# Two mixture-of-experts layers behind a windowed attention: the first weight matrix, the second group's softmax and the residues of the last two weight jobs are put in another order at the end of the preparation

## The chip, the cores and the metric

The kernel runs on one core of one Trainium2 chip. The time is device microseconds (us) of one execution; "the time before" is the median of three runs. A profile of one execution gives the rows below.

## What is computed

`x` is [2, 3584, 192]. Each token first gets a softmax-weighted mean over a window of seven rows (8 heads, `weight_gen`). Then a mixture of 8 experts with the best two of eight by noisy logits, then a second one with the best one by cosine similarity:

```python
w = exp(weight_gen - max); w = w / (sum(w) + 1e-9)
x = einsum('bshk,bskhg->bshg', w, windows_of(x))        # 7 rows back
for e in range(8):                                      # layer one, top 2 of 8
    h = maximum(x[mask] @ w1[e], 0); out[mask] += gate * (h @ w2[e])
# layer two: top 1 of 8, out[mask] = gate_w * (relu(x @ w1[e]) @ w2[e])
```

There are 7168 tokens, 192 features, 1024 hidden features. All inputs are fp32; the kernel forms fp16 pairs (a high part and a residue) to keep the precision.

## The kernel before, in words

**Stages.** The kernel has a head, in which no expert product runs, and a body, in which tiles of 256 tokens of one expert go through TensorE one after the other. The 56 columns of 128 tokens are cut into three groups: columns 0 to 24, 24 to 40 and 40 to 56. The head does the attention, the gate and the list of rows of the first group, and the preparation of layer one's weights. The attention and the lists of the other groups run on VectorE and ScalarE beside the tiles of the body.

**Weight jobs.** `prep_gen` (L308) prepares the weights of a layer in eight jobs of two experts each: four for the first matrix `w1` (m == 0) and four for the second matrix `w2` (m == 1). A job loads fp32 weights into one of three staging places (the end of `xh`, and the two weight buffers `wb`, called wb_134 and wb_133 in the built program), sums squares on ScalarE (`junk`), gets a scale `wsc` by a small matmul and VectorE steps (`wss`, `q`, `wsc`, `wiv`, `cinv`), and then for each half forms the high part on ScalarE (L395, `wo`) and the residue on VectorE (L397, `wo`). Each job of `w2` has four such pairs of 768 columns and two writes of 768 KB to the DRAM table `ws` (L404). The jobs are counted 0 to 7 here; job 5 uses wb_133, job 6 the end of `xh`, job 7 wb_134.

**First list.** `ctl` for the first group ends in `list_gen` (L835) and `decode` (L903): VectorE forms one-hot factors (`ol`, `ou`, `orr`), TensorE multiplies them (L875), VectorE reads the product (`dv`, L897) and goes by `va`, `dfv`, `sx`, `df` to the index table `gx` (L912). That last step is kept in `state["ctl"]`. GpSimd's indirect gathers of token rows (`xg`, L1123) wait for it.

**Second group's softmax.** `softmax_gen` (L433) does the largest of seven, subtraction, exponential on ScalarE (L442), sum, reciprocal and multiplication on `wt`. For the second group its first step is put behind `state["ctl"]`. Its input comes by `load_w(*G1[1])`, issued in the setup at priority `R_B`.

**First tile.** For each tile TensorE transposes the gathered rows (L1164, `pt`), ScalarE copies them (L1168, `xt`), and `first_product` (L1173) does four groups of ten matmuls into `ph`, a PSUM tile with three buffers. After each group ScalarE writes the high part `hh` (L1190) and VectorE the residue `hl` (L1191), which frees the `ph` buffer. Behind each half of the first tile's transposes, 18 small matmuls (`warm`, L1149) run. The second tile's transposes are issued behind the third group. `second_product` (L1198) then multiplies `hh` and `hl` by the second matrix into `py` (L1211).

**Weights of a tile.** `weights` (L1139) has SyncE read the expert number and a flag from tables in SBUF (`xi`, `fi`) and issue the load from `ws` into `wb` (L1147): part 0 is the first matrix (1024 KB), part 1 the second (768 KB). All loads and stores of SyncE stand in one queue, in the order in which it issues them; an issue that waits holds all issues behind it.

**What sets the order.** The kernel is written as generators that a queue steps; a scheduler orders the instructions of each engine by priorities (`p0 + R_CTL` is the most urgent; then `R_ATT`, `R_PREP`, `R_B`, `R_BODY`) and by `tc.issue_after`, which keeps an instruction behind a named one.

Of the kernel before, what the change touches and what calls it, by code (L numbers as in the profile page):

```python
# [12 lines left out]
ALU = mybir.AluOpType  # L13
AX = mybir.AxisListType

N, D, E, F, H, G, K = 7168, 192, 8, 1024, 8, 24, 7
# [3 lines left out]
G1 = ((0, 24), (24, 40), (40, 56))  # L20
# [7 lines left out]
CJ = 2  # L28
R_CTL, R_ATT, R_PREP, R_B, R_BODY = 0, 2000, 2000, 18000, 20000
C_AT = 5  # L30
R_LOW = 40000
P_STEPS = (0.5, 1.0)
SHARE = 0.845
ORDER = (0, 0, 1, 0, 1, 0, 1, 1)
# [51 lines left out]
def two_moe(ctx: ExitStack, tc: tile.TileContext, x, wgen, w_gate, w_noise, noise, w1a, w2a, emb, tau, w1b, w2b, out):  # L86
# [6 lines left out]
    WS = [[nc.dram_tensor(f"ws{i}{j}", (E * 128, n), F16, kind="Internal").ap() for j, n in enumerate((4096, WC - 4096))] for i in range(2)]  # L93
# [8 lines left out]
    V, A, PE, SP, PL = nc.vector, nc.scalar, nc.tensor, nc.sync, nc.gpsimd  # L102
# [28 lines left out]
    wr = wgen.rearrange("b s h k -> (b s) (h k)").rearrange("(p t) c -> p t c", t=NCOL)  # L131

    def load_w(a, b):
        SP.dma_start(wt[:, a:b].rearrange("p t h k -> p t (h k)"), wr[:, a:b])

    def load_x(a, b):
        SP.dma_start(xh[:, 6 + a:6 + b], xr[:, a:b])
# [140 lines left out]
    assert G1[0][1] * D >= 3072 and (G1[1][1] - G1[0][1]) * D >= 3072  # L278

    ready = set()  # L280

    @contextmanager
    def urgent(l):
# [9 lines left out]
    side, state = [], {"tile": 0}  # L293
# [14 lines left out]
    def prep_gen(l, w1, w2):  # L308
# [28 lines left out]
        for i, (e, m) in enumerate(jobs):  # L337
# [32 lines left out]
            n = 2  # L370
# [9 lines left out]
            for c in range(3 if m == 0 else 2):  # L380
                if len(wos) > 2 and any(f is wos[-3] for f, _ in side):
                    flush(True)
                wo = prep.tile([128, 3072], F16, name="wo", bufs=3)
                if m == 0:
                    n = 2048
                    w = 512 if l else 1024
                    pieces = [(wo[:, f:f + w], wo[:, 1024 + f:1024 + f + w], st[:, 1024 * c + f:1024 * c + f + w]) for f in range(0, 1024, w)]
                else:
                    n = 3072
                    wv = wo.rearrange("p (g a d) -> p g a d", a=2, d=D)  # L390
                    sv = st[:, 1536 * c:1536 * c + 1536].rearrange("p (g d) -> p g d", d=D)
                    w = 2 if l else 4
                    pieces = [(wv[:, g:g + w, 0], wv[:, g:g + w, 1], sv[:, g:g + w]) for g in range(0, 8, w)]
                for h, lo, v in pieces:
                    A.activation(h, v, AF.Copy, scale=sc[:, c:c + 1])  # L395
                    yield 0.1
                    V.scalar_tensor_tensor(lo, v, sc[:, c:c + 1], h, op0=ALU.mult, op1=ALU.subtract)  # L397
                    yield 0.6
                    if not l:
                        yield 0.1  # L400
                        yield 0.5
                def write(e=e, m=m, c=c, wo=wo, n=n):
                    if m == 1:
                        SP.dma_start(WS[l][1][(e + c) * 128:(e + c + 1) * 128], wo)  # L404
                    elif c < 2:
                        SP.dma_start(WS[l][0][(e + c) * 128:(e + c + 1) * 128, 0:2048], wo[:, 0:n])
                    else:
                        for q in range(4):
                            r = (e + q // 2) * 128 + 64 * (q % 2)
                            SP.dma_start(WS[l][0][r:r + 64, 2048:4096], wo[64 * (q // 2):64 * (q // 2) + 64, 0:n])  # L410

                wos.append(write)
                if l:
                    behind(write, 1)
                else:
                    write()
# [16 lines left out]
    def softmax_gen(a, b):  # L433
        n = (b - a) * H
        w = wt[:, a:b].rearrange("p t h k -> p (t h) k")
        m = ranks[1][0].rearrange("p e c -> p (e c)")
        with (tc.issue_after(state["ctl"].ins) if a == G1[1][0] else ExitStack()):
            V.tensor_reduce(m[:, :n], w, axis=AX.X, op=ALU.max)
        yield 6.0e-3 * n
        V.tensor_tensor(w, w, m[:, :n, None].to_broadcast([128, n, K]), op=ALU.subtract)  # L440
        yield 6.0e-3 * n
        A.activation(w, w, AF.Exp)  # L442
        yield 0.5
        V.tensor_reduce(m[:, :n], w, axis=AX.X, op=ALU.add)
        V.tensor_scalar(m[:, :n], m[:, :n], 1e-9, None, op0=ALU.add)
        V.reciprocal(m[:, :n], m[:, :n])
        yield 12.0e-3 * n
        V.tensor_mul(w, w, m[:, :n, None].to_broadcast([128, n, K]))
        yield 6.0e-3 * n

    state.update(accs=0, att=0)
# [671 lines left out]
            PL.indirect_dma_start(out=xg[:, h], out_offset=None, in_=T[l][0:rows_in],  # L1123
                                      in_offset=bass.IndirectOffsetOnAxis(ap=gidx[l][:, u + h:u + h + 1], axis=0))

    loads = []
    lone = [[i for i in seq if tiles[i][0] == l and tiles[i][4] == 1] for l in range(2)]

    def lone_weights(i):
# [43 lines left out]
    def first_product(i, bg):  # L1173

        l, L, pos, u, nh = tiles[i]
        c, w = slot(i)
        n = 128 * nh
        xm, xl, xr3 = live[i]["xt"]
        hh, hl = hidden[turn[i]]

        for g in range(4):
            ph = psum.tile([128, 2, 256], F32, name="ph", bufs=3)
            for q in range(2):
                f = 2 * g + q
                a, b, r, r2 = (w[:, o + 128 * f:o + 128 * f + 128] for o in (0, 1024, 2048, 3072))
                ops = ((a, xm), (a, xl), (b, xm), (r, xr3), (r2, xr3))
                for j, (s, m) in enumerate(ops):
                    state["pe"] = mark = PE.matmul(ph[:, q, :n], s, m, start=j == 0, stop=j == 4)  # L1188
            fs = slice(2 * g, 2 * g + 2)
            A.activation(hh[:, fs, :n], ph[:, :, :n], AF.Relu)  # L1190
            state["pin"] = V.scalar_tensor_tensor(hl[:, fs, :n], ph[:, :, :n], 0.0, hh[:, fs, :n], op0=ALU.max, op1=ALU.subtract)  # L1191
            bg(SHARE * nh / 2)
            if g == 2 and after.get(i) in live:
                with tc.issue_after(mark.ins):
                    transp(after[i])
            yield
        live[i]["h"] = (hh, hl)
# [88 lines left out]
    def att_gen(g):  # L1286
        a, b = L1.groups[g]
        while g and not ctl_done.get("h") or g == 2 and not state.get("last"):
            yield None
        cuts = [a, a + CH, b] if g == 0 else [a, b]  # L1290
        for u, v in zip(cuts, cuts[1:]):
            yield from softmax_gen(u, v)
        while g and head["on"]:
            yield None
        for c0 in range(a, b, CH):
            acc = yield from (att_chunk(c0) if g else att_chunk_pe(c0))
            bgq.chain(post_chunk(0, acc, c0, lgs[0][g], a, None, dones[0][g]))
        state["att"] += 1
# [127 lines left out]
    bgq.chain(prep_gen(0, w1a, w2a), "h", p0 + R_PREP)  # L1426
    load_x(2 * CH, GA)
    tc.cur_priority = p0 + R_B
    load_w(*G1[1])
    load_x(*G1[1])  # L1430
    tc.cur_priority = p0
    bgq.rank = p0 + R_CTL
# [4 lines left out]
        bgq.add(0, ctl(1, g, f"c{g}"), f"c{g}")  # L1437
    bgq.add(1, att_gen(0), "h", 0, p0 + R_ATT)
    for g in range(1, len(G1)):
        bgq.add(1, att_gen(g), f"s{g}")  # L1440
    bgq.add(1, emb_prep(), "c0")
    bgq.add(2, prep_rest(), "c0", 0, p0 + R_LOW)
    for g, (a, b) in enumerate(G2):
        bgq.add(1, combine_gen(g), f"c{g}", run_by(b))
    bgq.finish("h")
    head["on"] = False
    assert not locks["rows"]
    limit["rows"] = 1
# [33 lines left out]
        gather(i)  # L1482
    for part in range(2):
        for i in seq[:2]:
            weights(i, part)
    transp(0)
    for _ in first_product(0, bgq.point):
        pass
# [69 lines left out]
```

## Time and profile before

| | us |
|---|---|
| median of three runs | 1017.2 (1016.65 to 1022.86) |
| the profiled execution | 1016.67 |
| its span, first to last instruction | 1014.9 |
| TensorE busy in the span | 889.3 (88%) |
| VectorE busy | 682.5 (67%) |
| ScalarE busy | 572.3 (56%) |
| granted TensorE clock, mean | 0.963 of full |

The profiled execution took 1.77 us more than its span. In the rows, PE is TensorE's matmul, DVE is VectorE, ACT is ScalarE, POOL is GpSimd, SP is SyncE. A row of the timeline has the start from the beginning of the span, the duration, the engine and line, what is written and read, and in brackets the idle time before it and what ended that. Several instructions of one kind in succession are merged to one row (x4), with the time from the first's start to the last's end.

### The profile page before, as it was taken

How to read it: one execution, taken by the hardware profiler on the slowest of the kernel's cores; microseconds unless marked ns; L12 is line 12 of the kernel's file. 1: busy time of each engine (PE TensorE's matmuls, PEld its weight loads, DVE VectorE, ACT ScalarE, POOL GpSimd, SP SyncE). 2: the span in 40 equal slices, each digit the busy share in tenths (PEclk: the TensorE clock that was granted, in tenths of full speed). 3: DMA queues.
4: the chain of work that ended last, by engine and by line, in shares of the span. 5: the costliest groups of instructions: out<-in, count | busy, mean ns of one | idle time of the engine just before them, and what ended most of it. 6: DMA issues, size and time to landing. Idle time of an engine off the chain costs nothing. (4 is left out here: it accounts for less than half of the span.)

```text
span 1014.9 us, 26141 instructions
## 1 busy us (share of the span) xinstructions
PE 889.3 (88%) x9750; PEld 802.8 (79%) x9750; DVE 682.5 (67%) x1732; ACT 572.3 (56%) x1219; POOL 400.3 (39%) x379
## 2 busy tenths in 40 slices
PE   4993149999899999999899789899999989999995
PEld 2552139998889988889888688898898889999995
DVE  8996959998998958973457668275866663323331
ACT  2978526677557668356756774366357434434442
POOL 1000043454354544553544434354455334443532
PEclk9997559999999999999999999999999999999998
DMA  8789792856288584759999976782886657387650
GB/s 258 200 250 284 253 347 90 255 174 198 81 271 282 173 288 150 234 197 298 322 365 359 325 248 219 266 307 78 267 279 243 208 170 246 122 333 257 211 184 23
DMA packets 96393, 236.32 MB, mean 233 GB/s; under 512 B 13439, under 2 KB 64223, under 8 KB 87808
## 3 DMA queue, kind: packets, MB, share of 16 engines
q1 hardware_dynamic: 79360, 200.35, 58.0%
q0 software_dynamic: 16896, 34.20, 10.9%
q8 instruction: 79, 1.29, 0.5%
q14 instruction: 58, 0.48, 0.1%
HBM read 230.60 MB, written 57.90 MB: 284 GB/s over the span
## 5 line engine op out<-in xcount | busy, mean ns | idle before, releaser
L1188 PE MATMUL ph<-xt,wb 128*128 128x256 f16 x3360 | 413.6, 274 | 17.7 <-DMA wb<-ws 7.3
L1188 PEld LDWEIGHTS <-wb 128*128 128x128 f16 x3360 | 324.0, 98 | 57.1 <-issue 13.2
L1211 PE MATMUL py<-wb,hh 128*128 128x192 f16 x2688 | 357.5, 247 | 10.1 <-issue 5.4
L1190 ACT ACTIVATE hh<-ph 128x512 f16<-128x512 f32 (+1 forms) x368 | 209.3, 577 | 243.5 <-PE ph L1188 125.8
L1211 PEld LDWEIGHTS <-hh 128*128 128x128 f16 x2816 | 252.4, 98 | 20.5 <-issue 16.6
L1123 POOL DMA_INDIRECT xg<-t,gx x176 | 186.5, 1060 | 191.1 <-DVE gx L912 124.6
L1219 POOL DMA_INDIRECT yb<-ys,sx x116 | 130.8, 1128 | 250.9 <-ACT ys L1216 231.2
L1191 DVE SCALAR_TENSOR_TENSOR wt<-ph,hh 128x512 f16<-128x512 f32 x184 | 126.3, 688 | 144.5 <-ACT hh L1190 108.2
L1191 DVE SCALAR_TENSOR_TENSOR hl<-ph,hh 128x512 f16<-128x512 f32 (+1 forms) x184 | 117.6, 641 | 141.4 <-ACT hh L1190 113.3
L1211 PE MATMUL py<-wb,wt 128*128 128x192 f16 x736 | 181.9, 247 | 2.9 <-issue 2.9
L1211 PE MATMUL py<-wb,hl 128*128 128x192 f16 x608 | 149.5, 246 | 2.1 <-issue 2.0
L1219 POOL DMA_INDIRECT out_dram<-ys,sx x60 | 61.5, 1025 | 134.4 <-ACT ys L1216 120.5
L1216 ACT ACTIVATE ys<-py,xg 128x192 f32<-128x192 f32 x176 | 64.6, 415 | 64.3 <-PE py L1211 50.5
L465 DVE TENSOR_TENSOR tmp<-xh,wt 128x768 f32<-128x768 f32 x90 | 84.7, 951 | 1.4 <-PE ph L492 1.0
L1168 ACT ACTIVATE xt<-pt 128x768 f16<-128x768 f16 x84 | 67.9, 808 | 29.5 <-remote 12.3
L1211 PEld LDWEIGHTS <-wt 128*128 128x128 f16 x736 | 72.3, 98 | 3.8 <-issue 3.6
L1211 PEld LDWEIGHTS <-hl 128*128 128x128 f16 x672 | 65.7, 98 | 1.0 <-issue 0.9
L1164 PE MATMUL pt<-identh,xg 128*128 128x128 f16 x528 | 45.2, 220 | 11.1 <-DMA xg<-t,gx 9.7
L395 ACT ACTIVATE wo<-xh,wsc 128x384 f16<-128x384 f32 (+3 forms) x66 | 44.2, 716 | 12.5 <-DVE wsc L264 12.1
L397 DVE SCALAR_TENSOR_TENSOR wo<-xh,wsc,wo 128x384 f16<-128x384 f32 (+3 forms) x66 | 48.6, 744 | 2.9 <-ACT wo L395 2.8
L559 ACT ACTIVATE xt<-rb 128x768 f16<-128x768 f16 x56 | 43.4, 812 | 10.7 <-PE rb L553 4.9
L1164 PEld LDWEIGHTS <-xg 128*128 128x128 f16 x528 | 36.4, 98 | 13.6 <-DMA xg<-t,gx 10.3
(330 smaller groups left out, 918.3 us busy)
## 6 DMA issues: line engine op xcount, KB each, us to landing
wb<-ws SPq DMA_DIRECT2D x84, 1024.0 KB
wb<-ws SPq DMA_DIRECT2D x84, 768.0 KB
ws<-wo SPq DMA_DIRECT2D x16, 768.0 KB
tmp<-yb SPq DMA_DIRECT2D x28, 384.0 KB
ws<-wo SPq DMA_DIRECT2D x16, 512.0 KB
ws<-wo SPq DMA_DIRECT2D x32, 256.0 KB
xh<-ws SPq DMA_DIRECT2D x8, 1024.0 KB
xh<-in_moe_w_dram SPq DMA_DIRECT2D x10, 768.0 KB
```

The source lines that it names most:

```text
L395: A.activation(h, v, AF.Copy, scale=sc[:, c:c + 1])
L397: V.scalar_tensor_tensor(lo, v, sc[:, c:c + 1], h, op0=ALU.mult, op1=ALU.subtract)
L465: V.tensor_mul(dst.rearrange("p t (h g) -> p (t h) g", g=G), xv, w)
L1123: PL.indirect_dma_start(out=xg[:, h], out_offset=None, in_=T[l][0:rows_in], in_offset=bass.IndirectOffsetOnAxis(ap=gidx[l][:, u + h:u + h ...
L1164: mark = PE.transpose(pt[:, j, h], xg[:, h, 128 * b:128 * b + 128], identh)
L1168: A.activation(xt.rearrange("p j h n -> p (j h n)"), pt.rearrange("p j h n -> p (j h n)"), AF.Copy)
L1188: state["pe"] = mark = PE.matmul(ph[:, q, :n], s, m, start=j == 0, stop=j == 4)
L1190: A.activation(hh[:, fs, :n], ph[:, :, :n], AF.Relu)
L1191: state["pin"] = V.scalar_tensor_tensor(hl[:, fs, :n], ph[:, :, :n], 0.0, hh[:, fs, :n], op0=ALU.max, op1=ALU.subtract)
L1211: state["pe"] = PE.matmul(py[:, h], t[:, f, hs], w2[:, f, c], start=f == 0 and j == 0, stop=f == 7 and j == 2)
L1216: A.activation(ys[:, h], py[:, h], AF.Copy, scale=xg[:, h, 192:193].bitcast(F32))
L1219: d = PL.indirect_dma_start(out=dst, out_offset=bass.IndirectOffsetOnAxis(ap=sidx[l][:, u + h:u + h + 1], axis=0), in_=ys[:, h], in_offset ...
```

## The change

Six edits stand in the diff.
1. The residues of layer one's last two weight jobs (6 and 7) are held until the first list is there and put behind `state["ctl"]`. The last residue is kept as `state["wlast"]`.
2. The second group's softmax is put behind `state["wlast"]`, and starts only when layer one's weights are all prepared; all of it is written in the head, at the rank `R_SOFT`.
3. Its last multiplication is kept as `state["smax"]`, and the first tile's residues `hl` are put behind that.
4. The load of the second group's `weight_gen` columns is issued behind the write of job 5's second half, and stands in `loads`, the list behind whose last member the next weight load is put.
5. The first tile's first matrix is loaded at rank `R_CTL`, the other three loads of the first two tiles at `R_BODY + 1000`.
6. `loads` is made earlier, and `load_w` returns the instruction.

```diff
-R_LOW = 40000
+R_LOW, R_SOFT = 40000, 8000
...
     def load_w(a, b):
-        SP.dma_start(wt[:, a:b]...
+        return SP.dma_start(wt[:, a:b]...
...
+                    last = not l and i >= len(jobs) - 2
+                    while last and "ctl" not in state:
+                        yield None
+                    with tc.issue_after(state["ctl"].ins) if last else ExitStack():
+                        mark = V.scalar_tensor_tensor(lo, v, sc[:, c:c + 1], h, op0=ALU.mult, op1=ALU.subtract)
+                    if not l:
+                        state["wlast"] = mark
...
                     if m == 1:
-                        SP.dma_start(WS[l][1][(e + c) * 128:(e + c + 1) * 128], wo)
+                        mark = SP.dma_start(WS[l][1][(e + c) * 128:(e + c + 1) * 128], wo)
+                        if (l, e, c) == (0, 2, 1):
+                            with tc.issue_after(mark.ins):
+                                loads.append(load_w(*G1[1]))
...
-        with (tc.issue_after(state["ctl"].ins) if a == G1[1][0] else ExitStack()):
+        with (tc.issue_after(state["wlast"].ins) if a == G1[1][0] else ExitStack()):
             V.tensor_reduce(m[:, :n], w, axis=AX.X, op=ALU.max)
...
-        V.tensor_mul(w, w, m[:, :n, None].to_broadcast([128, n, K]))
+        state["smax"] = V.tensor_mul(w, w, m[:, :n, None].to_broadcast([128, n, K]))
...
-            state["pin"] = V.scalar_tensor_tensor(hl[:, fs, :n], ph[:, :, :n], 0.0, hh[:, fs, :n], op0=ALU.max, op1=ALU.subtract)
+            with tc.issue_after(state["smax"].ins) if i == seq[0] else ExitStack():
+                state["pin"] = V.scalar_tensor_tensor(hl[:, fs, :n], ph[:, :, :n], 0.0, hh[:, fs, :n], op0=ALU.max, op1=ALU.subtract)
...
+        while g and 0 not in ready:
+            yield None
         for u, v in zip(cuts, cuts[1:]):
             yield from softmax_gen(u, v)
+        state["soft"] = g
...
-    load_w(*G1[1])
...
-        bgq.add(1, att_gen(g), f"s{g}")
+        bgq.add(1, att_gen(g), f"s{g}", 0, p0 + R_SOFT)
...
     bgq.finish("h")
+    while state["soft"] < 1:
+        bgq.threads[1][0].step()
...
         for i in seq[:2]:
+            tc.cur_priority = p0 + (R_CTL if (i, part) == (seq[0], 0) else R_BODY + 1000)
             weights(i, part)
+    tc.cur_priority = p0 + R_BODY
```

**VectorE, end of the first list.** `wo<-xh` are residues of job 6, `dv` to `gx` the last steps of the list, `wss` the first scale step of job 7. Before:

```order
L885 TENSOR_TENSOR ou<-jtab,rhf 128x4x128
L397 SCALAR_TENSOR_TENSOR wo<-xh,wsc,wo 128x4x192
L886 TENSOR_TENSOR orr<-ou,vtab 128x4x128
L397 SCALAR_TENSOR_TENSOR wo<-xh,wsc,wo 128x4x192
L897 TENSOR_SCALAR dv<-ph 128x64
L397 SCALAR_TENSOR_TENSOR wo<-xh,wsc,wo 128x4x192
L1007 CAST va_186<-dv 128x64
L368 TENSOR_REDUCE wss<-pt 128x2
```

With the change (the lines are those of the changed file, ten or so further down):

```order
L895 TENSOR_TENSOR ou<-jtab,rhf 128x4x128
L896 TENSOR_TENSOR orr<-ou,vtab 128x4x128
L907 TENSOR_SCALAR dv<-ph 128x64
L1017 CAST va_186<-dv 128x64
L916 TENSOR_SCALAR dfv<-va_186 128x34
L919 CAST sx_172<-dfv 128x34
L920 TENSOR_SCALAR dfv<-dfv 128x34
L921 TENSOR_SCALAR df_1217<-dfv 128x34
L922 TENSOR_TENSOR gx_170<-dfv,df_1217 128x34
L402 SCALAR_TENSOR_TENSOR wo<-xh,wsc,wo 128x4x192 x4
L369 TENSOR_REDUCE wss<-pt 128x2
```

The four residues of job 6 moved from between the list's last steps to behind `gx`; job 7's four then follow, and the softmax (L448 to L458) follows those, ahead of the first `hl`.

**ScalarE, first tile.** `wo<-wb_134` are the high parts of job 7, `wt<-wt` is the softmax's exponential, `xt<-pt` the copies of the first and the second tile's transposes, `hh_190<-ph` the first tile's high parts. Before:

```order
L347 ACTIVATE junk,wnr<-wb_134 128x768
L395 ACTIVATE wo<-wb_134,wsc 128x4x192 x4
L442 ACTIVATE wt<-wt 128x896
L1168 ACTIVATE xt<-pt 128x768
L1190 ACTIVATE hh_190<-ph 128x512 x3
```

With the change:

```order
L396 ACTIVATE wo<-wb_134,wsc 128x4x192
L1177 ACTIVATE xt<-pt 128x768
L1199 ACTIVATE hh_190<-ph 128x512
L396 ACTIVATE wo<-wb_134,wsc 128x4x192
L1199 ACTIVATE hh_190<-ph 128x512 x2
L1177 ACTIVATE xt<-pt 128x768
L452 ACTIVATE wt<-wt 128x896
L1199 ACTIVATE hh_190<-ph 128x512
```

Two high parts of job 7 stand at each of the two L396 rows' places. Job 7's second half moved behind the first tile's first `hh`, and the exponential behind three `hh` and the second tile's `xt`.

**SyncE, first weight loads.** `ws<-wo` are the weight jobs' writes, `wb_133` takes the first tile's matrices, `wb_134` the second's. Before:

```order
L134 DMA wt<-in_weight_gen_dram 128x896
L404 DMA ws<-wo 128x3072 x2
L137 DMA xh<-in_x_dram 128x3072
L404 DMA ws<-wo 128x3072 x2
L1145 TENSOR_LOAD xi_166
L1147 DMA wb_133<-ws 128x4096
L1147 DMA wb_134<-ws 128x4096
L1147 DMA wb_133<-ws 128x3072
```

With the change (in both, the small register rows between the loads are left out):

```order
L134 DMA wt<-in_weight_gen_dram 128x896
L1154 TENSOR_LOAD xi_166
L1156 DMA wb_133<-ws 128x4096
L411 DMA ws<-wo 128x3072 x4
L137 DMA xh<-in_x_dram 128x3072
L1156 DMA wb_134<-ws 128x4096
L1156 DMA wb_133<-ws 128x3072
```

The first tile's first matrix moved ahead of four `ws` writes and the load of `x`; the load of `x` moved behind the last `ws` write, just ahead of the second tile's first matrix.

## Rows read from the trace of the kernel before

**Rows 1.** Waits of TensorE over the span (total us, times, longest).
```profile
PE pt L1164 <- DMA xg<-t,gx: 9.7, 1, 9.7
PE ph L1188 <- DMA wb<-ws: 7.3, 2, 6.1
```

**Rows 2.** Timeline of PE, 120 to 157 us.
```profile
125.04 0.59 PE L875 MATMUL ph<-orr,ol 128*128 128x64 bf16 x8 [1.95 <-DVE orr L886]
...
135.82 0.50 PE L1164 MATMUL pt<-identh,xg 128*128 128x128 f16 x3 [9.67 <-DMA xg<-t,gx]
...
137.87 1.65 PE L1154 MATMUL ph<-identh 128*128 128x96 f16 x18
145.64 6.23 PE L1188 MATMUL ph<-xt,wb 128*128 128x256 f16 x30 [6.12 <-DMA wb<-ws]
...
152.04 2.47 PE L1188 MATMUL ph<-xt,wb 128*128 128x256 f16 x20
...
156.43 0.82 PE L1188 MATMUL ph<-xt,wb 128*128 128x256 f16 x6
```

**Rows 3.** Timeline of DVE, 90 to 175 us.
```profile
122.38 1.01 DVE L397 SCALAR_TENSOR_TENSOR wo<-xh,wsc,wo 128x768 f16<-128x768 f32 x1
123.30 0.42 DVE L885 TENSOR_TENSOR ou<-jtab,rhf 128x512 bf16<-128x512 bf16 x1
...
125.83 0.22 DVE L897 TENSOR_SCALAR dv<-ph 128x64 int32<-128x64 int32 x1
...
128.00 0.20 DVE L912 TENSOR_TENSOR gx<-dfv,df 128x34 int32<-128x34 f32 x1
...
132.89 1.08 DVE L444 TENSOR_REDUCE rk<-wt 128x128 f32<-128x896 f32 x1
...
136.05 1.09 DVE L448 TENSOR_TENSOR wt<-wt,rk 128x896 f32<-128x896 f32 x1
148.62 0.69 DVE L1191 SCALAR_TENSOR_TENSOR hl<-ph,hh 128x512 f16<-128x512 f32 x1 [11.47 <-ACT hh L1190]
```

**Rows 4.** Timeline of ACT, 126 to 149 us.
```profile
127.62 3.42 ACT L395 ACTIVATE wo<-wb,wsc 128x768 f16<-128x768 f32 x4 [1.69 <-DVE wsc L264]
131.15 0.95 ACT L442 ACTIVATE wt<-wt 128x896 f32<-128x896 f32 x1
138.12 0.81 ACT L1168 ACTIVATE xt<-pt 128x768 f16<-128x768 f16 x1 [6.02 <-PE pt L1164]
147.99 0.60 ACT L1190 ACTIVATE hh<-ph 128x512 f16<-128x512 f32 x1 [9.06 <-PE ph L1188]
```

**Rows 5.** Timeline of SP's issues, 110 to 142 us (x2: first start to last end).
```profile
118.22 0.42 SPq L134 DMA_DIRECT2D wt<-in_weight_gen_dram  x1
124.68 2.66 SPq L404 DMA_DIRECT2D ws<-wo  x2
127.39 0.42 SPq L137 DMA_DIRECT2D xh<-in_x_dram  x1
...
132.07 3.22 SPq L404 DMA_DIRECT2D ws<-wo  x2
137.97 0.37 SPq L1147 DMA_DIRECT2D wb<-ws  x1
139.85 2.33 SPq L1147 DMA_DIRECT2D wb<-ws  x2
```

**Rows 6.** Timeline of POOL: the first gather.
```profile
128.49 1.14 POOL L1123 DMA_INDIRECT xg<-t,gx  x1 [124.56 <-DVE gx L912]
```

**Rows 7.** Windows: stretch, length, busy of PE, PEld, DVE, ACT, POOL, granted clock, DMA share, GB/s.
```profile
122.00:124.00 2.00, 0.58 (x8) 0.47 (x8) 2.00 (x5) 2.00 (x4) 0.00 (x0) 0.50 0.21 82
...
140.00:142.00 2.00, 0.00 (x0) 0.00 (x0) 0.00 (x0) 0.00 (x0) 1.41 (x2) 0.50 1.06 283
...
145.60:151.30 5.70, 5.66 (x27) 4.04 (x28) 2.68 (x4) 1.19 (x2) 0.00 (x0) 0.50 0.89 357
151.40:245.00 93.60, 93.60 (x1089) 88.49 (x1088) 89.40 (x150) 62.38 (x140) 44.08 (x36) 1.00 0.58 183
```

More of the change, by code (lines that the diff above doesn't have):

```diff
@@ L133, in load_w @@
     def load_w(a, b):
-        SP.dma_start(wt[:, a:b].rearrange("p t h k -> p t (h k)"), wr[:, a:b])
+        return SP.dma_start(wt[:, a:b].rearrange("p t h k -> p t (h k)"), wr[:, a:b])
     def load_x(a, b):
@@ L280, in two_moe @@
     ready = set()
+    loads = []
     @contextmanager
@@ L396, in prep_gen @@
                     yield 0.1
-                    V.scalar_tensor_tensor(lo, v, sc[:, c:c + 1], h, op0=ALU.mult, op1=ALU.subtract)
+                    last = not l and i >= len(jobs) - 2
[5 more added lines that the diff above has]
+                        state["wlast"] = mark
                     yield 0.6
@@ L1124, in gather @@
                                       in_offset=bass.IndirectOffsetOnAxis(ap=gidx[l][:, u + h:u + h + 1], axis=0))
-    loads = []
     lone = [[i for i in seq if tiles[i][0] == l and tiles[i][4] == 1] for l in range(2)]
```

## The prediction, made before the changed kernel ran

> **What bounds the kernel now.** The view of the waits comes first, since TensorE is busy for 88% of the span and its idle time is what can be won. Its two long waits on data are both at the hand-over from head to body: 9.7 us for the first gathered rows (`pt <- xg`) and 6.1 us for the first weights (`ph <- wb`) [rows 1]. The timeline of PE shows them one behind the other: the last product of the first list runs at 125.04, the transposes at 135.82, the warm-up ends at 137.87 + 1.65 = 139.5, and the first tile's product starts at 145.64 [rows 2]. The stretch from 125.6 to 145.6 holds 4 us of PE work.
>
> The other timelines say why. On DVE the index table `gx` comes at 128.00, with residues of job 6 among the list's last steps [rows 3]; the gather starts 0.49 us later [rows 6]. On SP the first matrix of the first tile is issued at 137.97, since it stands behind the weight jobs' last write, the second of the two issues that start at 132.07 and end at 135.29 [rows 5]. The windows show half clock (0.50) from the hand-over to 151.3, then full clock [rows 7]. From 151.4 to 245 us PE is busy without a gap that counts [rows 7], so whatever lead the first two tiles have there is carried on.
>
> **The change part by part.**
>
> *The list (edit 1).* A residue takes 123.30 - 122.38 = 0.92 us of DVE's time [rows 3]. Three of job 6 stand ahead of `dv`, one behind it. Without them the last two one-hot steps would run from 122.38 to about 123.1, TensorE's last eight matmuls take 0.59 [rows 2], and `dv` starts near 123.9 instead of 125.83, now bound by that product. From `dv` to `gx` it was 128.00 - 125.83 = 2.17, of which one residue goes: 1.2. So `gx` starts at 125.1, 2.9 us earlier, and the first gather at 125.6.
>
> *The gather.* Before, the transposes came 135.82 - 128.49 = 7.3 us after its start [rows 2, 6]. This trace has no row for that gather on a free queue. Two `ws` writes of 768 KB and the 1536 KB load of `x` were issued from 124.68 to 127.81 [rows 5], 3.1 MB, some 9 us of DMA at the 357 GB/s of a full stretch [rows 7], so the gather ran into them. Now one write of 768 KB goes out beside it, at about 127.2. The bounds are 1.1 (the gather's own time) and 7.3; I take 3.5, since the bytes ahead shrink by three quarters. Transposes then start at 129.1, and the warm-up ends 3.7 later, at 132.8.
>
> *The first matrix (edits 4 and 5).* Its issue follows the `wt` load, 118.22 + 0.42, and the register reads, which took 137.97 - 135.29 = 2.7 [rows 5]: 121.3. DMA is nearly empty there, 82 GB/s between 122 and 124 [rows 7]. The 448 KB of `wt` and 1024 KB at 357 GB/s take 4.2, so it lands by 126, and the 6.1 us wait for weights is gone. What is late next is the gather and ScalarE's copy `xt`. The copy now stands behind job 7's first two high parts. Those need `wsc`, behind job 6's four residues: 125.3 + 3.7 + 0.6 (three dependent steps of 0.2, as `gx`) = 129.6, and 2 x 0.86 (a quarter of 3.42, [rows 4]) end at 131.3. The copy waits for both, about equally long, and the product starts at 133.0, 12.6 us earlier than at 145.64.
>
> *What gives most of it back (edits 1 to 3).* The first `hl` is now behind the softmax, and on ScalarE the exponential stands behind `hh` one to three and the second tile's `xt`, with job 7's second half behind the first `hh`. TensorE's fourth group needs the buffer that the first `hl` frees. Step by step: a group takes 6.23 / 3 = 2.1 at half clock, so `hh` one runs at 135.2 to 135.8; job 7's two high parts to 137.5; DVE forms their residues to 138.6, then two softmax steps of 1.0 each to 140.6. ScalarE meanwhile does `hh` two and three (the third group ends at 139.3), then the second `xt` at 140.0 to 140.8. The exponential follows (0.95), to 141.8. The four steps behind it took 136.05 + 1.09 - 132.89 = 4.25 with one residue between them, 3.3 without [rows 3]: 145.1. With 0.7 for the first `hl`, the fourth group starts at 145.9, against 152.04 [rows 2]. Of 12.6 us, 6.1 are left, and TensorE is idle from 139.8 to 145.9.
>
> *The weights behind it.* Job 7's last write is issued when its last residue is done, 138.7; then comes the load of `x` (0.42), then the second tile's first matrix, 2.7 later, then the first tile's second matrix 1.9 later (139.85 - 137.97). The queue holds 0.79 + 1.57 + 1.05 = 3.4 MB up to the second tile's first matrix and 4.2 MB with the next. At 360 GB/s (the better of the two full windows, 283 and 357 [rows 7]) and with 1 us from issue to movement, they land at 149.2 and 151.4. Before, the load of `x` was out of the way by 135.
>
> *The clock.* Before, the product ran at half clock from 145.64 to 151.3, after 6.1 us of idle [rows 2, 7]. I take the same for the fourth group, since it too follows a gap of 6 us. Then: fourth group 145.9 to 148.0, wait for weights to 149.2, first group of the second tile to 151.3, full clock from about 152, second group to 152.8, twelve `py` matmuls to 153.8. The third group of the second tile starts at 153.8 instead of 156.43 [rows 2]: 2.6 us earlier. The Trainium skill says, in "TensorE: Matmul & The Clock Gate", section "Why this matters for your kernels", that an idle gap between bursts of matmuls sends the array back to half clock; it speaks against this change, which cuts the first product in two. The trace agrees, with 0.50 after the idle 139.5 to 145.6. Were the clock full throughout, the second matrix at 151.4 would bind and the lead be 4.0; were it half to 155, the lead would be 1.
>
> *The rest.* VectorE's lead at the first `hl` is 148.62 - 145.1 = 3.5, more than 2.6, so it does not become the bound. The order of later work stays: the second list's `gx` stands behind 63 residues `hl` instead of 62, the third's behind 123 in both. I cost that at nothing; TensorE's products hide it, and it is worth 2 us either way if they don't. Edit 6 costs nothing.
>
> The sum is 1016.67 (the profiled execution, 0.5 under the median of 1017.2) - 2.6 = 1014.1 us.
>
> **The rivals.**
> 1. *The whole head start stays.* If something lets the exponential run early, all 12.6 us are won: 1004.1. The early product and the free queue at 122 speak for it; the order on ScalarE, where the exponential stands behind the third `hh`, speaks against it, and no engine reorders its own list.
> 2. *Slower, by the late gather.* If the gather takes its old 7.3 us, the transposes start at 132.9 and the product at 136.8. Job 7's second half hangs on the first `hh`, so its last write moves to 142.5, and the load of `x` and both weight loads behind it: the second matrix lands at 155.2. At half clock twelve `py` end at 157.2 to 158.6, 0.8 to 2.2 later than 156.43, so 1017.5 to 1018.9; I put it at 1018.2. It decides once the product starts after about 135.5. For it: one write beside the gather, and 283 GB/s in one window, by which the same loads take 14.8 us. Against: three quarters of the old traffic is gone.
> 3. *Nothing is left.* The lead of 2.6 is lost where a list or a weight load ends later than TensorE: 1016.7. For it: the list of the second group runs on a VectorE that is nearly full; against: all that hangs on it moved forward too.
>
> **How the numbers follow.** Forecast 0.55, with its own range 1011.5 to 1016.0 (leads of 1 to 5); rival 1 0.07, rival 2 0.20, rival 3 0.18. The likeliest is 1014.1. The range goes up to 1020, rival 2 with a microsecond of scatter, and down to 1008, the fourth group's full 6.1 and 2 us further on; less than 0.2 is left out. A measurement of this kernel tells about 1%, 10 us, from no change: faster than that only if most of rival 1 holds, 0.05; slower by that needs more than any mechanism here prices, 0.03; within it 0.92.
>
> **What would show it right or wrong.** Right: the first matrix issued near 121 and no wait of `ph` on it; `gx` near 125.1; the product from 133; a PE gap of 5 to 7 us ahead of the fourth group, ended by `hl` or VectorE's softmax; a short wait on `wb` ahead of the second tile; the second tile's third group at 153 to 155. Wrong: a product without that gap (rival 1), transposes near 133 (rival 2), or a lead at 156 that is gone by 300 us (rival 3).

## The result and the profile after

The changed kernel takes 1026.35 us (median of 20 runs, 1021.05 to 1029.9), the kernel before on the same chip 1020.52 (20 runs, 1016.65 to 1022.86): ratio 1.0064, 95% interval 1.0051 to 1.0077. It is slower by 0.6%, where 1014.1 and a gain of 2.6 us were forecast. The profiled execution of before, 1016.67, stands at the fast end of these 20, the fastest of which took 1016.65; from their median the same sum would have given 1020.5 - 2.6 = 1017.9.

The waits of TensorE in the changed kernel's span (total us, times, longest), beside [rows 1]:

```profile
PE ph L1197 <- DVE hl L1201: 11.1, 2, 7.8
...
PE ph L1197 <- DMA wb<-ws: 5.4, 2, 2.8
...
PE pt L1173 <- DMA xg<-t,gx: 3.9, 2, 2.6
```

The 9.7 us for gathered rows and the 6.1 us for the first matrix are gone. A wait of 7.8 us for `hl` has come, and the group of the wait for rows has two members: 1.23 us in the first tile, and one of 2.6 us that stands far from the change. The timeline of PE, for [rows 2]:

```profile
128.03 0.50 PE L1173 MATMUL pt<-identh,xg 128*128 128x128 f16 x3 [3.31 <-DVE wss L369]
...
131.21 0.50 PE L1173 MATMUL pt<-identh,xg 128*128 128x128 f16 x3 [1.23 <-DMA xg<-t,gx]
...
132.94 4.90 PE L1197 MATMUL ph<-xt,wb 128*128 128x256 f16 x30
...
145.97 2.29 PE L1197 MATMUL ph<-xt,wb 128*128 128x256 f16 x10 [7.78 <-DVE hl L1201]
150.89 4.43 PE L1197 MATMUL ph<-xt,wb 128*128 128x256 f16 x20 [2.63 <-DMA wb<-ws]
...
156.74 1.25 PE L1197 MATMUL ph<-xt,wb 128*128 128x256 f16 x10
...
305.08 0.60 PE L1173 MATMUL pt<-identh,xg 128*128 128x128 f16 x6 [2.64 <-DMA xg<-t,gx]
```

The product (132.94) and its fourth group (145.97) start within 0.1 us of the forecast. The second tile's third group then comes at 156.74, against 156.43 before: no lead is left. And at 305 TensorE waits 2.64 us for rows that the second list should have brought; before waits for rows only once, in the first tile [rows 1]. The timeline of DVE, for [rows 3]:

```profile
123.99 0.20 DVE L922 TENSOR_TENSOR gx<-dfv,df 128x34 int32<-128x34 f32 x1
...
136.77 1.95 DVE L402 SCALAR_TENSOR_TENSOR wo<-wb,wsc,wo 128x768 f16<-128x768 f32 x2 [5.43 <-ACT wo L396]
138.63 1.08 DVE L448 TENSOR_REDUCE rk<-wt 128x128 f32<-128x896 f32 x1
...
145.23 0.68 DVE L1201 SCALAR_TENSOR_TENSOR hl<-ph,hh 128x512 f16<-128x512 f32 x1
145.83 0.95 DVE L475 TENSOR_TENSOR acc<-xh,wt 128x768 f32<-128x768 f32 x1
...
150.23 0.95 DVE L475 TENSOR_TENSOR tmp<-xh,wt 128x768 f32<-128x768 f32 x1
153.84 0.69 DVE L1201 SCALAR_TENSOR_TENSOR wt<-ph,hh 128x512 f16<-128x512 f32 x1 [2.67 <-ACT hh L1199]
```

VectorE stands idle for 5.43 us ahead of the last two residues of the weights and for 2.67 us ahead of the second tile's first residue (written to the free place `wt`, fifth residue of the body). Between the first and the fifth it does four steps of the second group's attention (L475, L490).

SP's issues, for [rows 5], POOL's first gather, for [rows 6], and windows, for [rows 7]:

```profile
116.79 0.42 SPq L134 DMA_DIRECT2D wt<-in_weight_gen_dram  x1
120.53 0.36 SPq L1156 DMA_DIRECT2D wb<-ws  x1
126.08 13.00 SPq L411 DMA_DIRECT2D ws<-wo  x4
139.13 0.42 SPq L137 DMA_DIRECT2D xh<-in_x_dram  x1
142.47 5.92 SPq L1156 DMA_DIRECT2D wb<-ws  x4
```
```profile
124.48 1.64 POOL L1133 DMA_INDIRECT xg<-t,gx  x1 [120.56 <-DVE gx L922]
```

```profile
135.60:139.60 4.00, 2.58 (x25) 2.16 (x24) 2.83 (x3) 2.56 (x5) 2.40 (x3) 0.96 0.31 82
139.60:150.90 11.30, 2.31 (x11) 1.36 (x11) 10.15 (x14) 2.82 (x4) 0.00 (x0) 0.64 1.00 387
139.60:154.00 14.40, 5.41 (x25) 3.57 (x25) 10.58 (x15) 3.41 (x5) 0.00 (x0) 0.61 0.89 348
145.90:156.40 10.50, 7.81 (x39) 5.56 (x39) 7.26 (x11) 1.79 (x3) 0.00 (x0) 0.50 0.62 257
```

DMA moves 82 GB/s between 135.6 and 139.6: the queue is nearly empty while the last `ws` write waits for its residues, and the load of `x` and three weight loads stand behind that write. The granted clock is 0.96 of full from 135.6 to 139.6, ahead of TensorE's gap, and half from the fourth group behind that gap to 156.4.

### The profile page after: what moved, and what is told of

Same layout as the page of the kernel before. It is cut to its first block, busy times and chain, and to the rows that moved or that the text cites. A ratio compares the mean times of both kernels' runs of the same rounds, so it can differ in the third digit from the quotient of the medians.

```text
span 1024.5 us, 26142 instructions
## 1 busy us (share of the span) xinstructions
PE 896.3 (87%) x9750; PEld 808.6 (79%) x9750; DVE 683.4 (67%) x1732; ACT 571.6 (56%) x1219; POOL 397.2 (39%) x379
## 4 chain that ended last, share of the span: by engine, by line
PE 57%; DVE 17%; ACT 9%; DMA 8%; issue 5%; SPq 1%; another core or an unknown queue 1%; POOL 1%; ACTq 0%; POOLq 0%; DVEq 0%
PE ph L1197 26%; PE py L1221 24%; DMA wb<-ws 4%; PE pt L1173 2%; DVE wo L402 2%; DVE wt L1201 2%; ACT hh L1199 2%; DVE tmp L475 2%; ACT wo L396 2%; ACT junk L348 2%; DVE hl L1201 2%; PE rb L563 1%; DMA ws<-wo 1%; PE py L502 1%
## 5 line engine op out<-in xcount | busy, mean ns | idle before, releaser
L1229 POOL DMA_INDIRECT yb<-ys,sx x116 | 128.7, 1109 | 275.5 <-ACT ys L1226 251.0
L475 DVE TENSOR_TENSOR tmp<-xh,wt 128x768 f32<-128x768 f32 x90 | 84.2, 950 | 0.6 <-PE ph L502 0.6
L396 ACT ACTIVATE wo<-xh,wsc 128x384 f16<-128x384 f32 (+3 forms) x66 | 44.2, 719 | 12.2 <-DVE wsc L264 12.1
L490 DVE TENSOR_TENSOR acc<-acc,tmp 128x768 f32<-128x768 f32 x48 | 45.7, 953 | 0.4
```

Of the source, the lines that this page charges most:

```text
L475: V.tensor_mul(dst.rearrange("p t (h g) -> p (t h) g", g=G), xv, w)
L1229: d = PL.indirect_dma_start(out=dst, out_offset=bass.IndirectOffsetOnAxis(ap=sidx[l][:, u + h:u + h + 1], axis=0), in_=ys[:, h], in_offset ...
```

## The experiments

Four groups of runs, each on one chip with its own runs of before; medians of before: 986.64, 985.07, 1020.04 and 1026.4 us. Only ratios are compared between groups.

**First group: which edit makes the gap, and does the loss lie at the hand-over or behind it?**

`base_again` is before, unchanged.

> The kernel before, unchanged, for one more profile. Theory H (hand-over: the change loses its head start between 140 and 157 us, and what is lost later is scatter of the first profile of before, which was 3.8 us under the median): this profile is near 1020, and its later tiles stand 2 to 4 us behind those of the first profile. Theory B (body: the change disturbs the later lists and the clock, and loses 4 to 7 us beyond tile 5): this profile's later tiles stand where the first profile has them, within 1 us, and its time is 1016 to 1018.

One run: 984.08 us. This chip is 3% faster than that of the first profile, so its time tells nothing on that profile's scatter; its trace serves as before's for the first two groups, whose chips are about as fast as each other. Its head does tell something. The `wt` load, which stands right behind job 5's last write, is issued here at

```profile
116.62 0.42 SPq L134 DMA_DIRECT2D wt<-in_weight_gen_dram  x1
```

and at 116.2 to 117.5 in all other traces, but at 118.22 in the profile from which the prediction was made [rows 5]: that head was 1.4 us later than the changed kernel's.

`nosmax` is the changed kernel without edit 3:
```diff
-            with tc.issue_after(state["smax"].ins) if i == seq[0] else ExitStack():
+            with ExitStack():
```


> The changed kernel without edit 3 (the first tile's residues hl no longer stand behind the softmax); all else as changed. Theory H: the 7.8 us gap ahead of the fourth group goes, the fourth group runs by 142; the second tile still waits for its first matrix, which lands near 150 behind the last ws write and the load of x, so the third group of the second tile starts 1 to 3 us earlier than 156.7 and the time is 1023 to 1025, still not under before. Theory B: what is lost after tile 5 stays whole, 1025 to 1027.

Ratio 1.0044 (1.0022 to 1.0065), 989.35 us. The fourth group ran at 137.84 without a wait, the second tile's third group came at 154.7 (156.2 in the changed kernel on a chip as fast); TensorE stood 10.84 us for the second tile's matrix. In PE's and DVE's timelines:

```profile
149.93 3.97 PE L1197 MATMUL ph<-xt,wb 128*128 128x256 f16 x20 [10.84 <-DMA wb<-ws]
```
```profile
152.89 0.69 DVE L1201 SCALAR_TENSOR_TENSOR wt<-ph,hh 128x512 f16<-128x512 f32 x1 [4.04 <-ACT hh L1199]
```

The gap of 7.8 us had mostly hidden the wait for the matrix; most of the loss stays without edit 3 (1.0044, with an interval that overlaps the changed kernel's).

`unbind` is the changed kernel without edit 1:
```diff
-                    last = not l and i >= len(jobs) - 2
+                    last = False
```


> The changed kernel without edit 1 (the residues of the last two weight jobs are free to run between the list's steps, as before); edits 2 to 6 stay. Theory H: gx is back near 128, the product starts 2 to 4 us later than 132.9, but job 7's writes and the load of x are out of the queue by 145, so the second tile starts within 1 us of where it does with the change; time within 2 us of the changed kernel, 1024 to 1028. Theory B: if the held residues are what disturbs the body, the time falls to 1018 to 1022.

Ratio 1.0049 (1.0026 to 1.0072). Without the holding of the residues the loss stays too.

`first_x` (before with edits 4 to 6, and the load of `x` right behind the `wt` load):
```diff
+                            with tc.issue_after(loads[-1].ins):
+                                loads.append(load_x(*G1[1]))
...
-    load_x(*G1[1])
```


> The kernel before with edits 4 to 6 alone (early load of the second group's weight_gen columns and of the first tile's first matrix), and the load of x issued right behind the weight_gen load; softmax, residues and hl as before. Theory H: no wait for the first matrix, the softmax ahead of the first tile, no gap inside the first product: the second tile's third group starts 4 to 9 us before 156.4 and most of that stays to the end, 1012 to 1017. Theory B does not speak against this, since the second list and the softmax are as before: 1012 to 1017 too. A third theory (N: whatever the head wins is lost again in the body, which waits for lists that do not come earlier): 1019 to 1022.

Ratio 1.0005 (0.9989 to 1.0022): the third theory's number. But the reason is seen in the hand-over itself. ScalarE and TensorE:

```profile
137.27 0.60 ACT L1195 ACTIVATE hh<-ph 128x512 f16<-128x512 f32 x1 [1.91 <-PE ph L1193]
137.77 1.75 ACT L396 ACTIVATE wo<-wb,wsc 128x768 f16<-128x768 f32 x2
```
```profile
149.00 4.42 PE L1193 MATMUL ph<-xt,wb 128*128 128x256 f16 x20 [8.15 <-DMA wb<-ws]
```

Job 7's second half stands behind the first `hh`, so the buffer wb_134 comes free late, and the second tile waits for its matrix.

After this group theory H stood for the hand-over (the matrix is late in each of the three), but it didn't give the size: `nosmax` came out at the upper end of what it allowed. The loss behind it needed a theory of its own.

**Second group: is it VectorE's chain to the second list?**

`after_again` is the changed kernel.

> The changed kernel once more, beside before on one chip. What the two theories say of the place of the loss, from the run without edit 3: theory V (VectorE's chain to the second list is what the body waits for: softmax, attention, gate and list of the second group; the change starts the attention at the same time but lets VectorE stand behind the second tile's first residue, which waits for its late first matrix): the second group's gx comes 4 to 7 us later than before's on the same chip, TensorE waits 2 us and more for xg or the list's VectorE steps between 275 and 320 us, and the ratio is 1.004 to 1.007. Theory B (the order deeper in the body is disturbed): gx of the second list within 2 us of before's, the loss spread over many waits.

Ratio 1.0057 (1.0037 to 1.0078). The second list's `gx` and the transposes that need it, in `base_again` and in this run, with the first products of the sixteenth and the eighteenth tile around them:

```profile
284.50 2.35 PE L1188 MATMUL ph<-xt,wb 128*128 128x256 f16 x20
...
290.97 0.18 DVE L912 TENSOR_TENSOR gx<-dfv,df 128x32 int32<-128x32 f32 x1
...
299.04 0.50 PE L1164 MATMUL pt<-identh,xg 128*128 128x128 f16 x6
...
303.94 2.35 PE L1188 MATMUL ph<-xt,wb 128*128 128x256 f16 x20
```
```profile
285.22 2.35 PE L1197 MATMUL ph<-xt,wb 128*128 128x256 f16 x20
...
295.52 0.20 DVE L922 TENSOR_TENSOR gx<-dfv,df 128x32 int32<-128x32 f32 x1
...
301.03 0.60 PE L1173 MATMUL pt<-identh,xg 128*128 128x128 f16 x6 [2.33 <-DMA xg<-t,gx]
...
306.70 2.34 PE L1197 MATMUL ph<-xt,wb 128*128 128x256 f16 x20
```

`gx` is 4.5 us later, and the wait for rows is there again. At the sixteenth tile the changed kernel was only 0.7 us behind; at the eighteenth it is 2.8 behind. So the second list costs about 2.0 us.

`xearly` (the changed kernel, with the same two lines as `first_x` for the load of `x`):

> The changed kernel with the load of x issued right behind the weight_gen load, so that 1.5 MB leave the queue ahead of the second tile's first matrix; the softmax and residues as changed. Theory V: the second tile's first matrix lands near 146 instead of 150, VectorE's idle time ahead of the second tile's first residue (2.7 us) goes, the second list's gx comes 2 to 4 us earlier, and the time falls by 2 to 4 us, to a ratio of 1.001 to 1.004 against before. Theory B: no change in the later tiles, ratio as with the change, 1.004 to 1.007.

Ratio 0.9991 (0.9975 to 1.0006), 983.9 us, 6 us better than the changed kernel beside it and better than expected. So where the load of `x` stands decides as much as the whole loss. TensorE didn't wait for the second tile's matrix, nor VectorE for the second tile:

```profile
144.00 6.04 PE L1199 MATMUL ph<-xt,wb 128*128 128x256 f16 x30 [5.99 <-DVE hl L1203]
```
```profile
149.12 0.69 DVE L1203 SCALAR_TENSOR_TENSOR wt<-ph,hh 128x512 f16<-128x512 f32 x1
```

With `x` early, edits 1 to 3 together cost nothing that can be told (0.9991 beside the 1.0005 of `first_x`).

The second tile's third group came at 150.9, 3.2 us ahead of before's 154.1. At the sixteenth tile 2.6 us of that lead were left, at the eighteenth almost nothing (303.7 against 303.9), since the wait for rows stayed:

```profile
PE pt L1175 <- DMA xg<-t,gx: 2.6, 1, 2.6
```

`first_xh` (as `first_x`, and the first tile's copy bound behind job 7's last high part, kept as `state["high"]`):
```diff
+            with tc.issue_after(state["high"].ins) if i == seq[0] else ExitStack():
                 A.activation(xt..., pt..., AF.Copy)
```


> The kernel with early loads of weight_gen, x and the first matrix, the rest as before (1.0005 against before), with one binding more: the first tile's copy xt on ScalarE stands behind the last high part of job 7, so that job 7's second half no longer stands behind the first hh. Theory V: job 7's last write is issued near 136 instead of 141, the second tile's first matrix lands at 142 to 145 instead of 148.6, VectorE's wait of 4.5 us at 148 goes, the second list's gx comes 3 to 5 us earlier, and the time is 3 to 5 us under before, ratio 0.995 to 0.997. Theory N (the head start is lost in any case): ratio 0.999 to 1.002.

Ratio 0.9977 (0.9962 to 0.9991): faster than both kernels. ScalarE and TensorE:

```profile
130.55 1.74 ACT L396 ACTIVATE wo<-wb,wsc 128x768 f16<-128x768 f32 x2
135.06 0.81 ACT L1176 ACTIVATE xt<-pt 128x768 f16<-128x768 f16 x1 [2.77 <-PE pt L1171]
```
```profile
144.76 3.22 PE L1196 MATMUL ph<-xt,wb 128*128 128x256 f16 x28 [3.68 <-DMA wb<-ws]
```

One binding on ScalarE moved the matrix 4 us forward. The second `gx` came at 284.3, 6.7 us before 291.0, and the lead of 6.7 us stayed through the list; at the end of the traced run 4.4 us of it were left.

`vadd` (before, at the start of the second group's attention):
```diff
+        for k in range(3 if g == 1 else 0):
+            tap(att.tile([128, CH, D], F32, name="tmp", bufs=4), a, k)
```


> The kernel before with three more multiplications of 0.95 us on VectorE (dead results in the tmp buffers) behind the first tile's first residue, where the second group's attention begins; loads, softmax and lists as before. They add 2.6 us to VectorE's chain to the second list and leave TensorE's first tiles nearly alone. Theory V: the second list's gx is 2 to 3 us later and the time grows by 2 to 3 us, ratio 1.002 to 1.003. If the chain had slack (the sum of the prediction, which took VectorE's lead as enough): ratio within 0.001 of 1.

Ratio 1.0018 (1.0003 to 1.0033), the second `gx` 2.0 us later. 2.6 us put on VectorE there cost about 2 us at the end. The lag is there from the second tile on (1.8 us at its third group), and `gx` comes as far behind the sixteenth tile as in before (6.4 us): what has no slack is VectorE beside the first tiles, which holds up the tiles themselves.

**Third group.** `first_only` is before with edits 4 to 6, `first_xh_again` is `first_xh` ("the faster version") once more, `first_xh1` is that with edit 1, `xearly_e` is `xearly` with the second `hh` of the first tile behind the exponential.

> The kernel before with edits 4 to 6 alone (early weight_gen load, early first matrix); x, softmax, residues and hl as before. Theory V: the first product starts 5 to 8 us earlier, but the second tile's first matrix, behind job 7's last write, lands at 147 to 150 as before or later, VectorE waits 2 to 5 us ahead of the second tile's first residue, and the ratio is 0.999 to 1.002. By the prediction's sum (the lead of the first two tiles is kept): ratio 0.994 to 0.997.

> The faster version once more, to see whether its gain repeats. Theory V: ratio 0.995 to 0.999, second gx 4 us and more before 291. If the first comparison was luck: 0.999 to 1.002.

> The faster version plus edit 1 (residues of jobs 6 and 7 behind the first list's last step; softmax and hl as before). gx comes 2.5 us earlier. Theory V: VectorE does the same work in another order and the second tile's first matrix still hangs on job 7's last write, issued within 1.5 us of where it was; the second gx moves by less than 2 us either way and the ratio stays at 0.996 to 0.999. If the first list were what binds: 0.993 to 0.996.

> The changed kernel with the early load of x, and the second of the first tile's hh on ScalarE put behind the softmax's exponential on request (edit: hh of the second group stands behind the exponential). As built the exponential still stands behind two hh and the second tile's xt on ScalarE, one hh earlier than in the run with early x alone. Theory V: VectorE's wait of 2.5 us for the exponential shrinks by 0.5 to 1, the second gx by as much, ratio 0.998 to 1.000, that is not to be told from the run with early x (0.9991).

0.9967 (0.9948 to 0.9986), 0.9948 (0.9928 to 0.9967), 0.9968 (0.9946 to 0.9991) and 1.0016 (0.9995 to 1.0038). The faster version's gain repeats, and edit 1 adds nothing to it (its second `gx` was 3.4 us later than without, more than the 2 expected). `first_only` missed my expectation: edits 4 to 6 alone win a little here (in the fourth group, 0.9988, it can't be told from before). `xearly_e` came out on the other side of 1 than expected, with intervals that overlap; it decides nothing.

**Fourth group: edit 1 or edit 2?** `only1` has edits 1, 4, 5, 6, `only2` 2, 4, 5, 6, beside `first_only_b` (4 to 6) and `after_c` (all).
```diff
-        with (tc.issue_after(state["wlast"].ins) if a == G1[1][0] else ExitStack()):
+        with (tc.issue_after(state["ctl"].ins) if a == G1[1][0] else ExitStack()):
...
-        while g and 0 not in ready:
-            yield None
...
-        bgq.add(1, att_gen(g), f"s{g}", 0, p0 + R_SOFT)
+        bgq.add(1, att_gen(g), f"s{g}")
...
-    while state["soft"] < 1:
-        bgq.threads[1][0].step()
```
(for `only1`, with the line of `nosmax`; `only2` has the lines of `unbind` and `nosmax`).

> Edits 1, 4, 5, 6: the residues of the last two jobs held behind the first list; the softmax bound as before, hl free. If edit 2 (softmax behind the last residue) carries the loss: the softmax's exponential stands ahead of xt on ScalarE, the load of x between the ws writes, the second list's gx stands behind 62 residues hl again and the ratio is 0.996 to 1.000. If edit 1 carries it: 1.003 to 1.006.

> Edits 2, 4, 5, 6: the softmax behind the last weight residue and written in the head; the residues of jobs 6 and 7 free as before, hl free. If edit 2 carries the loss: the softmax runs after 138 us, VectorE stands 3 to 5 us ahead of the second tile's first residue with nothing ahead of it done, gx behind 63 residues, ratio 1.003 to 1.006. If edit 1 carries it: 0.996 to 1.000.

> Edits 4 to 6 alone once more, beside the two runs above on one chip. The theory that edits 4 and 5 win a little and edits 2 and 3 lose it: 0.996 to 1.000. By the first reading of VectorE's chain, which expected no gain without an early second matrix: 0.999 to 1.002.

> The changed kernel beside the others on one chip: 1.004 to 1.008.

0.9985 (0.9959 to 1.0011), 1.0040 (1.0018 to 1.0062), 0.9988 (0.9962 to 1.0015) and 1.0064 (1.004 to 1.0087). Edit 2 carries most of the loss (1.0040 beside 0.9988), edit 1 none that can be measured; what edits 1 and 3 add to edit 2 (1.0064 beside 1.0040) is within the intervals.

Two things change with edit 2. The first is the place of the load of `x`. In `only1` it stands between job 6's and job 7's writes, in `only2`, as in the changed kernel, behind the last of them:

```profile
128.94 0.42 SPq L137 DMA_DIRECT2D xh<-in_x_dram  x1
```
```profile
137.49 0.42 SPq L137 DMA_DIRECT2D xh<-in_x_dram  x1
```

The second tile's third group came at 152.61 in `only1` and at 155.34 in `only2`, 2.7 us later; 1.9 of that were left at the sixteenth tile. The second is the order on VectorE. What it does ahead of the fifth residue, in `only1` and in `only2`:

```profile
143.90 0.94 DVE L475 TENSOR_TENSOR tmp<-xh,wt 128x768 f32<-128x768 f32 x1
151.09 0.69 DVE L1201 SCALAR_TENSOR_TENSOR wt<-ph,hh 128x512 f16<-128x512 f32 x1 [6.25 <-ACT hh L1199]
```
```profile
149.02 0.96 DVE L475 TENSOR_TENSOR acc<-xh,wt 128x768 f32<-128x768 f32 x1
149.90 1.82 DVE L475 TENSOR_TENSOR tmp<-xh,wt 128x768 f32<-128x768 f32 x2
151.63 0.95 DVE L490 TENSOR_TENSOR acc<-acc,tmp 128x768 f32<-128x768 f32 x1
152.50 0.68 DVE L1201 SCALAR_TENSOR_TENSOR wt<-ph,hh 128x512 f16<-128x512 f32 x1
```

`only1` has six attention steps behind it and waits 6.25 us, as its next instruction is that residue; `only2` has four. Counted in the traces of all kernels that ran:

| | without edit 2 (10 traces) | with edit 2 (8 traces) |
|---|---|---|
| attention steps ahead of the fifth residue | 6 (`vadd`: 6 and its 3 dead ones) | 4 |
| residues ahead of the second list's `gx` | 62 | 63 |
| `gx` behind the sixteenth tile's first product matmul | 6.4 to 6.6 us | 10.3 to 10.4 us |
| TensorE's wait for the rows of that list | none | 2.3 to 2.8 us |
| from the sixteenth tile's first product to the eighteenth's, faster chips (4 traces each) | 19.4 us | 21.5 to 22.0 us |
| the same, slower chips (6 and 4 traces) | 21.2 to 21.6 us | 21.7 to 23.6 us |

The third line doesn't depend on how early the tiles are: `first_xh` with a lead of 6.7 us and `vadd` with a lag of 2 have the same 6.4, `xearly` with a lead of 3.2 the same 10.3 as the changed kernel. VectorE goes through one fixed list, in which attention and list steps stand at set places between the residues. Counted residue by residue, the changed kernel's row of background steps is mostly one or two behind that of before, up to the list. That the two steps missing at the start push the whole row back is the likeliest reading, but it isn't shown: which part of edit 2 sets that order (the binding, the wait for all weights or the rank, which also holds for the attention steps) was not tried.

The lag of TensorE against `base_again` in five traces of the faster chips (us; a lead is negative; single traces):

| | second tile, third group | sixteenth tile | eighteenth tile | end of the span |
|---|---|---|---|---|
| `after_again` | 2.1 | 0.7 | 2.8 | 4.7 |
| `nosmax` | 0.6 | 1.0 | 3.2 | 2.3 |
| `xearly` | -3.2 | -2.6 | -0.3 | -0.5 |
| `first_x` | 0.2 | 0.7 | 0.7 | 1.5 |
| `first_xh` | -7.2 | -6.7 | -6.7 | -4.4 |

The three kernels with edit 2 lose 2.0 to 2.4 us across the second list, the two without it nothing. The lag at the second tile comes from the hand-over.

## Why the prediction was right or wrong

- **The list, the first matrix, the product: right, and the last tenths by luck.** `gx` at 123.99 (forecast 125.1), first matrix issued at 120.53 (121.3), product at 132.94 (133.0), first `hl` at 145.23 (145.1), fourth group at 145.97 (145.9). The gather took at most 128.03 - 124.48 = 3.55 us for the 3.5 chosen (the row of the transposes gives VectorE's `wss` as the end of their wait). The 12.6 us became 6, as said. But the times were worked out from a head that was 1.4 us later. Counted from the `wt` load, 116.79 here and 118.22 in [rows 5], the product came 1.4 us later than forecast and the fourth group 1.5. The steps took 1.4 us longer than forecast, and the head of this run was 1.4 us earlier: the two cancelled.
- **The weights behind it: mis-sized.** The forecast let 3.4 MB go at 360 GB/s and had the second tile's matrix at 149.2; TensorE went on with it at 150.89, 1.7 us later. The rate was not the error. From 139.6 to 150.9 the DMA engines moved 387 GB/s, 4.4 MB: the loads issued behind that matrix moved beside it, and the forecast had counted only the bytes up to it. Over 139.6 to 154.0 it was 348 GB/s.
- **The clock: mis-sized.** The 0.50 after the gap was forecast; its end was put at 152, and it lasted to 156.4, which made the work from 150.89 to 156.74 take 1.25 us more than forecast. The Trainium skill ("TensorE: Matmul & The Clock Gate", section "Why this matters for your kernels") says that an idle gap between bursts of matmuls brings half clock back, and this trace agrees: 0.96 over 135.6 to 139.6, 0.50 over 145.9 to 156.4. The trace of before could not show it, since its clock was 0.50 ahead of the gap too (122 to 124 in [rows 7]).
- **The lead of 2.6 us was not there.** These two terms turned it into a lag of 0.3 here (1.7 counted from the `wt` load), and of 2.1 us in `after_again` (156.2 against 154.1). `xearly` shows that the load of `x` behind the last write cost it: without that the lead was 3.2.
- **The rest: the step that failed.** "the second list's `gx` stands behind 63 residues `hl` instead of 62 ... I cost that at nothing; TensorE's products hide it, and it is worth 2 us either way if they don't." They don't: `gx` is 3.8 us later against the tiles (10.3 for 6.5), TensorE waits 2.3 to 2.8 us for the rows in every run with edit 2, and the tiles lose 2.0 to 2.5 us there on the faster chips. The 2 us that the prediction named and left out of its sum were the right size. "VectorE's lead at the first `hl` is 148.62 - 145.1 = 3.5, more than 2.6, so it does not become the bound" failed with it: the first residue was early, but two attention steps were missing behind it, and VectorE stood 2.67 us idle ahead of the fifth.
- **The rivals.** Rival 3 (a list on a nearly full VectorE) named the place, but its price ended at no loss; rival 2 named slower, by a late gather that didn't come. The loss is a third thing: rival 3's mechanism with the sign of rival 2.
- **What stays open.** In `after_again` the lag was 0.7 us at the sixteenth tile, 2.8 at the eighteenth, 3.6 at the thirty-third and 4.7 at the end. Why the lag of the second tile shrank up to the sixteenth, and what the last 2 us are, was not traced; the latter is no more than the traces of other kernels drift there (`first_xh` lost 2.3, `nosmax` won 0.9).

## What to carry to other kernels

Where two engines work through fixed lists that are interleaved, count what stands between the marks that both share. Here the second list's end, one residue further back, stayed 10.3 us behind the tiles whether these came early (`xearly`) or late. An early load can lose its gain to the next load in the same queue, so follow the second tile's matrix as well as the first's, and read which release it waits for: the place of one load (`x`) was worth 6 us. And a binding that only reorders one engine (`xt` behind job 7's last high part) brought that matrix 4 us forward, and its kernel was faster than before on both chips that ran it.

## What the runs showed of the hardware

The same program took 985 to 987 us on two chips and 1020 to 1026 on others, 4% apart. Part of it is idle time of TensorE that ended with nothing that the profile shows (`issue`): the first profile of before has 26 such waits ahead of `py` alone, 10.4 us,

```profile
PE py L1211 <- issue: 10.4, 26, 1.1
```

and the same view of `base_again`, on a faster chip, lists none. All ten traces of the slower chips list such waits, none of the eight of the faster ones; their cause is open. The ratios of one change agreed across chips (1.0064, 1.0057, 1.0064); those of two smaller ones less so (0.9977 and 0.9948; 0.9967 and 0.9988).
